# Cluster attention and two MLPs: the preparation of a pair of heads spread to one matmul tile per unit, a second place for the queries' low parts, a third output buffer, and mask halves on two engines

## The chip, the cores and the metric

The kernel runs on one core of a Trainium2 chip. The metric is the time of one execution on the device in microseconds (us). Three executions of the kernel before are shown with their median; one more was profiled.

## The reference, cut to what matters

```python
def _attn_ref(q, k, v, centroids):                    # q, k, v: 2 x 8 x 768 x 64, 16 centroids per head
    q_n, k_n, c_n = (each divided by its norm + 1e-06)
    q_assign = np.argmax(np.einsum('bhsd,hcd->bhsc', q_n, c_n), axis=-1)
    k_assign = np.argmax(np.einsum('bhsd,hcd->bhsc', k_n, c_n), axis=-1)
    mask = q_assign[:, :, :, None] == k_assign[:, :, None, :]
    scores = scale * np.matmul(q, k.transpose(0, 1, 3, 2))
    scores = np.where(mask, scores, -1000000000.0)
    attn = softmax(scores)                            # with 1e-9 added to the sum
    return np.matmul(attn, v)

x = attention as 1536 x 512
x = (sigmoid(x @ w_gate) * (x @ w_val)) @ w_out       # d_ff 1536
x = relu(x @ w_in) ** 2 @ w_out2                      # d_ff 2048
```

A query attends to the keys of its own cluster alone, and the cluster is the centroid of the greatest similarity. Everything is computed to nearly fp32 accuracy: a matrix is held as a high part that TensorE takes in one pass (type F32R) and a low part, the rest.

## The kernel before, in words

The work before the MLPs is 8 pairs of heads (two heads of one batch entry), and each pair is 12 **units**: a head e (two), a half n of the queries (two), and a block j of 128 queries (three). In this text a unit's number is its place in its pair, 0 to 11; the program counts them through, 0 to 95 (`n` in the loop at line 885), and `UPP` is 12.

In a turn of the loop the engines get, in this order: DVE the row maximum of unit n (line 894, `nm<-s`); the copies (`post`) left by the turn before; PE the six transposes of the probabilities of unit n-3 (line 791, `t<-ident,p`), which ACT takes as high parts (793) and DVE as low parts (799, `pt_lo`); PE the scores of unit n+1 (773, `s`); ACT the exponentials (915); DVE the reciprocal of the row sums (844, `nm`) and POOL the normalisation (845, `p`). Then come a third of an attend (`o`, 809 and 810: four matmuls), every third turn with an output copy by ACT (815, `oc`), the sum and split of two heads' outputs on POOL (`finish`: 829, 838 `x_hi`, 840 `x_lo`), the parts of v on POOL (`values`), and last what the tables say for this turn. The matmul tiles of p's transposes and of all preparation come from one pool of three (`ps_t`, name `t`); scores have two, and `o` has one. Each engine works its instructions in the order of this program.

The **preparation** of pair i runs while earlier pairs are in their units. Its pieces are named: `tk0`, `tk1`, `tq0`, `tq1` transpose a half of keys or queries (three transposes, line 551; the high part by ACT, line 556; the low part by DVE, line 557); `s0`, `s1` are four matmuls against the centroids (614); `b0`, `b1` transpose the similarities back (631) and add two of them (641); `am` the maximum over centroids (652), `eq` the comparison with it on DVE (659) and a product on POOL (662), `oh` and `on` a second maximum and the one-hot (669, 675); `mk` six narrow transposes of the one-hot (685), from which ACT makes the row of the mask (695), and DMAs put the row into the operands of the scores (700). `ka`, `kb`, `qa`, `qb` are DMAs that copy parts between the stacked operands of the two heads (596, 600, 602); `load` fetches the inputs of the next pair. All DMAs go out on SP's queue.

`STEPS` names the turn of each piece, counted from the turn ahead of which pair i-1 has its unit 0; `SECOND_STEPS` is for pair 1, and its negative turns stand in the preparation of pair 0, behind its last eight of 17 pieces. A number of -8 to -1 is thus a unit 4 to 11 two pairs ahead of the prepared pair, and 0 to 9 a unit of the pair ahead of it. The low part of the queries has a place of its own (`lo_t["q"]`, from `low_tile`), in one input tile of the MLPs (`x_hi` of the last group) for pairs 0 to 5, and in a tile `lo_q` for pairs 6 and 7. DMAs `qa` and `qb` and the similarities read it. The output copy `oc0` of the first head is held until `finish` has made x_lo of it, some ten units later. Decoding of the first two weights (`early`) is spread over units of the first pairs, on DVE, ACT and POOL.

The stacked operands of pair i and pair i-2 are the same tiles.

Of the kernel before, what the change touches and what calls it, by code (L numbers as in the profile page):

```python
# [8 lines left out]
F32 = mybir.dt.float32  # L9
# [4 lines left out]
AF = mybir.ActivationFunctionType  # L14
ALU = mybir.AluOpType
# [13 lines left out]
STEPS = {  # L29
    -8: ["tq0"],  # L30
    -7: ["tk0"],
    -6: ["tk1"],
    -5: ["tq1", "s0"],
    -3: ["b0", "load"],
    -2: ["s1"],
    -1: ["kb"],
    0: ["qb", "b1"],
    1: ["am"],
    2: ["ka", "qa"],
    3: ["eq"],  # L40
    6: ["oh", "on"],
    7: ["mk"],
}

SECOND_STEPS = {
    -8: ["tk0"],
    -7: ["tq0"],
    -6: ["tk1", "s0"],
    -3: ["tq1"],
    -1: ["s1", "b0"],  # L50
    0: ["b1", "load"],
    1: ["kb"],
    2: ["qb"],
    4: ["am", "ka", "qa"],
    6: ["eq"],
    7: ["oh", "on"],
    9: ["mk"],
}

# [10 lines left out]
def cluster_attention_two_mlps(  # L70
# [13 lines left out]
    nc = tc.nc  # L84
    B, H, S, D = q.shape
    NCL = centroids.shape[1]
    P = 128
# [6 lines left out]
    NH = HB * P  # L94
    NPAIR = H // 2
    scale = 1.0 / float(D) ** 0.5
    TG = 512
    NG = B * S // TG
# [11 lines left out]
    x_in = x_tiles()  # L110
# [199 lines left out]
    with tc.manual_schedule():  # L310
# [12 lines left out]
        rscale = const.tile([4 * NCL, 1], F32, name="rscale")  # L323
        nc.gpsimd.memset(rscale[: 2 * NCL], -1.0)
        nc.gpsimd.memset(rscale[2 * NCL :], -BIG)
        rbias = const.tile([4 * NCL, 1], F32, name="rbias")
# [118 lines left out]
        with ExitStack() as ac:  # L445
# [3 lines left out]
            am = pc.enter_context(tc.tile_pool(name="am", bufs=1, side="right"))  # L449
# [4 lines left out]
            sm = ac.enter_context(tc.tile_pool(name="sm", bufs=6))  # L454
# [78 lines left out]
            Q, K, V = {}, {}, {}  # L533
            factor = {"q": scale, "k": 1.0}

            def prep(i):
# [42 lines left out]
                def low_tile():  # L579
                    if i < len(pairs) - 2:  # L580

                        return x_in[NG - 1][0].rearrange("p k t -> p (k t)")[:, :S]
                    if "hl" not in pools:
                        assert decoded[0] == EARLY and not any(x < N - UPP for x in decoding)
                        early_stack.close()
                        pools["hl"] = sc.enter_context(tc.tile_pool(name="hl", bufs=1))
                    return pools["hl"].tile([P, S], F32R, name="lo_q")
# [94 lines left out]
                def mask():  # L682
                    mt = ps_t.tile([4 * NCL, S], BF16, name="t")
                    for c in range(NB):
                        nc.tensor.transpose(mt[:, c * P : (c + 1) * P], keep["oh"][:, c, :], identb)

                    def post():
                        if i == 0:

                            for t, x in ((K, slice(0, NCL)), (Q, slice(2 * NCL, 3 * NCL))):  # L690
                                nc.scalar.activation(
                                    out=t[i, 0][D : D + NCL, 1], in_=mt[x], func=AF.Identity, scale=rscale[x], bias=rbias[x]
                                )
                        row = am.tile([4 * NCL, S], F32R, name="row")
                        nc.scalar.activation(out=row, in_=mt, func=AF.Identity, scale=rscale, bias=rbias)
                        for e in range(0 if i > 0 else 1, 2):
                            for t, tensor in enumerate((K, Q)):
                                r = slice((2 * t + e) * NCL, (2 * t + e + 1) * NCL)
                                at = D - NCL if e else D
                                nc.sync.dma_start(out=f32(tensor[i, e][at : at + NCL, 1]), in_=f32(row[r]))  # L700

                    return post
# [98 lines left out]
            def attend(i, e, n, third):  # L801

                if third == 0:
                    outs[i, e, n] = ps_o.tile([P, NH], F32, name="o")
                o = outs[i, e, n]
                hi, lo = PThi[i, e, n], PTlo[i, e, n]
                for c in range(third * NB // 3, (third + 1) * NB // 3):
                    vt = V[i, e][:, c].rearrange("p t d -> p (t d)")
                    nc.tensor.matmul(o, vt, hi[:, c, :], start=(c == 0), stop=False)  # L809
                    nc.tensor.matmul(o, vt, lo[:, c, :], start=False, stop=(c == NB - 1))  # L810
                if third == 2:

                    def post():
                        oc = sm.tile([P, NH], F32, name=f"oc{e}", bufs=2)
                        nc.scalar.copy(oc, outs.pop((i, e, n)))  # L815
                        own, other = slice(D * e, D * e + D), slice(D - D * e, 2 * D - D * e)
                        if e == 0:
                            xs[n] = [oc, sm.tile([P, NH], F32, name="x", bufs=2)]
                        nc.sync.dma_start(out=xs[n][1][own], in_=oc[other])
                        if e == 1:  # L820
                            nc.sync.dma_start(out=xs[n][0][own], in_=oc[own])

                    return post
# [61 lines left out]
            for n in range(N + LAG + 4):  # L885
# [10 lines left out]
                if nm is not None:  # L896
                    p = Pt[units[n - 1]]
# [15 lines left out]
                if u is not None:  # L913
                    e = pp.tile([P, S], F32, name="p")
# [92 lines left out]
```

## Time and profile before

| what | value |
|---|---|
| three executions, median (all) | 859.29 us (859.0, 859.29, 859.41) |
| the profiled execution, its own time | 857.28 us |
| its span, first to last instruction | 855.5 us |
| busy in the span: PE, DVE, ACT, POOL | 95%, 73%, 52%, 25% |
| granted TensorE clock, mean | 0.99 |

Engines: PE is TensorE, DVE VectorE, ACT ScalarE, POOL GpSimd, SP the engine whose queue issues the DMAs. The shares are means over attention and MLPs together. "idle before <-X" in a row is the time that the engine stood idle ahead of this instruction and what it then waited for. PE's ends are modelled, so that its busy times overlap.

### The profile page before, as it was taken

How to read it: one execution, taken by the hardware profiler on the slowest of the kernel's cores; microseconds unless marked ns; L12 is line 12 of the kernel's file. 1: busy time of each engine (PE TensorE's matmuls, PEld its weight loads, DVE VectorE, ACT ScalarE, POOL GpSimd, SP SyncE). 2: the span in 40 equal slices, each digit the busy share in tenths (PEclk: the TensorE clock that was granted, in tenths of full speed). 3: DMA queues.
4: the chain of work that ended last, by engine and by line, in shares of the span. 5: the costliest groups of instructions: out<-in, count | busy, mean ns of one | idle time of the engine just before them, and what ended most of it. 6: DMA issues, size and time to landing. Idle time of an engine off the chain costs nothing.

```text
span 855.5 us, 11621 instructions
## 1 busy us (share of the span) xinstructions
PE 816.7 (95%) x4069; PEld 693.1 (81%) x4069; DVE 626.2 (73%) x1143; ACT 446.6 (52%) x888; POOL 213.6 (25%) x347
## 2 busy tenths in 40 slices
PE   6698999999999999999999999999999999999998
PEld 5587988988989878788888888887878888888886
DVE  4598898889888647873678756797675688688533
ACT  6577788888888423343233222344654642652630
POOL 3467888888788110000000000000000000000000
PEclk9799999999999999999999999999999999999999
DMA  5635643643421212121222121211222212222012
GB/s 130 141 70 123 156 103 85 146 106 91 102 68 53 72 47 68 66 81 35 74 74 68 55 66 58 74 50 50 74 75 67 82 49 74 81 68 74 25 50 98
DMA packets 63274, 67.01 MB, mean 78 GB/s; under 512 B 28624, under 2 KB 54224, under 8 KB 63216
## 3 DMA queue, kind: packets, MB, share of 16 engines
q1 hardware_dynamic: 63216, 66.27, 28.2%
q8 instruction: 32, 0.52, 0.3%
q14 instruction: 26, 0.21, 0.1%
HBM read 45.12 MB, written 3.15 MB: 56 GB/s over the span
## 4 chain that ended last, share of the span: by engine, by line
PE 72%; DVE 13%; POOL 5%; ACT 4%; issue 3%; DMA 2%; SPq 0%; DVEq 0%; POOLq 0%; ACTq 0%
PE bank_b L418 16%; PE bank_a L341 12%; PE bank_a L342 12%; PE bank_a L340 12%; PE bank_a L418 9%; DVE pt_lo L799 3%; PE s L773 3%; PE t L791 3%; DVE nm L894 3%; POOL p L845 3%; PE o L809 2%; PE o L810 2%; POOL x_lo L840 1%; DMA st_q<-st_q 1%; PE t L614 1%
## 5 line engine op out<-in xcount | busy, mean ns | idle before, releaser
L342 PE MATMUL bank_a<-x_hi,w 128*128 128x512 f32 x480 | 187.7, 391 | 2.1 <-DVE w L228 2.1
L341 PE MATMUL bank_a<-x_lo,w 128*128 128x512 f32 x480 | 189.3, 394 | 0.3 <-POOL x_lo L840 0.3
L340 PE MATMUL bank_a<-x_hi,w 128*128 128x512 f32 x480 | 188.0, 392 | 0.0
L799 DVE TENSOR_TENSOR pt_lo<-t,pt_hi 128x384 fp32r<-128x384 f32 x192 | 97.6, 545 | 21.7 <-ACT pt_hi L793 20.9
L342 PEld LDWEIGHTS bank_a<-x_hi,w 128*128 128x128 f32 x480 | 90.1, 188 | 22.7 <-DVE w L228 2.5
L340 PEld LDWEIGHTS bank_a<-x_hi,w 128*128 128x128 f32 x480 | 90.1, 188 | 21.0
L341 PEld LDWEIGHTS bank_a<-x_lo,w 128*128 128x128 f32 x480 | 90.1, 188 | 20.4 <-POOL x_lo L840 0.8
L845 POOL TENSOR_SCALAR p<-p,nm,ones 128x768 f32<-128x768 f32 x96 | 96.6, 1006 | 26.5 <-DVE nm L844 24.9
L384 DVE TENSOR_TENSOR slo<-act,shi 128x512 fp32r<-128x512 f32 x84 | 57.4, 687 | 59.1 <-ACT shi L383 54.6
L915 ACT ACTIVATE p<-s,nm 128x768 f32<-128x768 f32 x96 | 88.2, 919 | 16.2 <-DVE nm L844 7.7
L773 PE MATMUL s<-st_k,st_q 128*128 128x384 f32 (+1 forms) x384 | 93.7, 367 | 1.5 <-ACT p L915 0.8
L894 DVE TENSOR_REDUCE nm<-s 128x1 f32<-128x768 f32 x96 | 90.8, 946 | 4.3 <-PE s L773 4.2
L791 PE MATMUL t<-ident,p 128*128 128x128 f32 x576 | 84.5, 281 | 5.5 <-DVE pt_lo L799 3.0
L793 ACT CAST pt_hi<-t 128x384 fp32r<-128x384 f32 x192 | 84.4, 490 | 10.1 <-PE t L791 8.8
L791 PEld LDWEIGHTS t<-ident,p 128*128 128x128 f32 x576 | 69.0, 144 | 14.0 <-ACT sim L620 2.9
L418 PE MATMUL bank_b<-wo,shi 128*128 128x512 f32 x256 | 79.3, 390 | 0.5 <-DVE wo L228 0.5
L383 ACT CAST shi<-act 128x512 fp32r<-128x512 f32 x84 | 51.2, 615 | 52.1 <-PE bank_b L418 27.1
L222 ACT CAST w<-wtop 128x512 fp32r<-128x512 f32 x38 | 23.7, 623 | 102.8 <-DVE wtop L240 102.8
L809 PE MATMUL o<-pt_hi,vt 128*128 128x384 f32 x192 | 66.8, 348 | 7.3 <-ACT oc L815 7.3
L366 DVE TENSOR_TENSOR act<-bank_a,sg 128x512 f32<-128x512 f32 x36 | 24.9, 690 | 66.4 <-PE bank_a L342 60.4
L773 PEld LDWEIGHTS s<-st_k,st_q 128*128 128x128 f32 (+1 forms) x384 | 64.9, 196 | 3.2 <-ACT p L915 1.8
L810 PE MATMUL o<-pt_lo,vt 128*128 128x384 f32 x192 | 65.6, 342 | 0.0
(129 smaller groups left out, 1378.8 us busy)
## 6 DMA issues: line engine op xcount, KB each, us to landing
wraw<-in_moe_w_out_dram SPq DMA_DIRECT2D x28, 512.0 KB, 3.3
wraw<-in_moe_w_in_dram SPq DMA_DIRECT2D x16, 512.0 KB, 3.8
wraw<-in_moe_w_gate_dram SPq DMA_DIRECT2D x11, 512.0 KB, 3.6
wraw<-in_moe_w_val_dram SPq DMA_DIRECT2D x11, 512.0 KB, 3.7
nat_v<-in_v_dram SPq DMA_DIRECT2D x8, 384.0 KB, 3.2
st_k<-st_k SPq DMA_DIRECT2D x16, 192.0 KB, 4.7
x<-oc SPq DMA_DIRECT2D x32, 96.0 KB, 2.1
out_dram<-part SPq DMA_DIRECT2D x12, 256.0 KB, 2.1
```

The costliest lines, as they stand in the source:

```text
L340: nc.tensor.matmul(bk, w[:, 0, ks], mov_hi[:, kk], start=(kk == 0), stop=False)
L341: nc.tensor.matmul(bk, w[:, 0, ks], mov_lo[:, kk], start=False, stop=False)
L342: nc.tensor.matmul(bk, w[:, 1, ks], mov_hi[:, kk], start=False, stop=(kk == KD - 1))
L418: nc.tensor.matmul(bk, st, mv, start=(first and n == 0), stop=(last and n == 2))
L773: nc.tensor.matmul(st[:, m, :NH], Q[i, e][: DEPTH[e][a], a, c * P : (c + 1) * P], K[i, e][: DEPTH[e][a], a, m * NH : (m + 1) * NH], start= ...
L791: nc.tensor.transpose(tp[:, m, :], Pt[u][:, c * P : (c + 1) * P], ident)
L793: nc.scalar.copy(hi, tp)
L799: nc.vector.tensor_tensor(out=lo, in0=tp, in1=f32(hi), op=ALU.subtract)
L809: nc.tensor.matmul(o, vt, hi[:, c, :], start=(c == 0), stop=False)
L845: nc.gpsimd.tensor_scalar(out=p, in0=p, scalar1=nm[:, 3:4], scalar2=ones, op0=ALU.mult, op1=ALU.mult)
L894: nc.vector.tensor_reduce(out=nms[n][:, 0:1], in_=st[n][:, :, :NH], axis=AX.XY, op=ALU.max, negate=True)
L915: nc.scalar.activation(out=e.rearrange("p (m n) -> p m n", m=2), in_=st.pop(n)[:, :, :NH], func=AF.Exp, bias=nms[n][:, 0:1], accum_out=nms ...
```

## The change

The two tables are rewritten, so that no turn has two pieces that take a tile of `ps_t`, and pair 1 has less in front of the first unit and more in units 0 to 5. The low parts of the queries alternate between two tiles for pairs 0 to 5 (`x_hi` and `x_lo` of the last group). Of the two mask halves of pair 0, that of the queries is made on DVE, by a multiplication (its bias is 0), while ACT makes that of the keys. The first head's output copies have three buffers, the second's two as before.

```diff
--- before.py
+++ after.py
@@ -29,31 +29,30 @@
 STEPS = {
     -8: ["tq0"],
     -7: ["tk0"],
-    -6: ["tk1"],
-    -5: ["tq1", "s0"],
+    -6: ["s0"],
+    -5: ["tk1"],
+    -4: ["tq1"],
     -3: ["b0", "load"],
     -2: ["s1"],
-    -1: ["kb"],
-    0: ["qb", "b1"],
-    1: ["am"],
-    2: ["ka", "qa"],
-    3: ["eq"],
-    6: ["oh", "on"],
-    7: ["mk"],
+    -1: ["kb", "b1"],
+    0: ["qb", "am"],
+    1: ["eq"],
+    2: ["oh", "on", "ka", "qa"],
+    3: ["mk"],
 }
 
 SECOND_STEPS = {
-    -8: ["tk0"],
-    -7: ["tq0"],
-    -6: ["tk1", "s0"],
-    -3: ["tq1"],
-    -1: ["s1", "b0"],
-    0: ["b1", "load"],
-    1: ["kb"],
-    2: ["qb"],
-    4: ["am", "ka", "qa"],
+    -6: ["load"],
+    -3: ["tk0"],
+    -2: ["tq0"],
+    -1: ["tk1"],
+    0: ["s0", "tq1"],
+    1: ["s1"],
+    2: ["b0", "kb"],
+    3: ["b1", "qb"],
+    5: ["am"],
     6: ["eq"],
-    7: ["oh", "on"],
+    7: ["oh", "on", "ka", "qa"],
     9: ["mk"],
 }
 
@@ -579,7 +578,7 @@
                 def low_tile():
                     if i < len(pairs) - 2:
 
-                        return x_in[NG - 1][0].rearrange("p k t -> p (k t)")[:, :S]
+                        return x_in[NG - 1][i % 2].rearrange("p k t -> p (k t)")[:, :S]
                     if "hl" not in pools:
                         assert decoded[0] == EARLY and not any(x < N - UPP for x in decoding)
                         early_stack.close()
@@ -687,10 +686,14 @@
                     def post():
                         if i == 0:
 
-                            for t, x in ((K, slice(0, NCL)), (Q, slice(2 * NCL, 3 * NCL))):
-                                nc.scalar.activation(
-                                    out=t[i, 0][D : D + NCL, 1], in_=mt[x], func=AF.Identity, scale=rscale[x], bias=rbias[x]
-                                )
+                            x = slice(2 * NCL, 3 * NCL)
+                            nc.vector.tensor_scalar(
+                                out=Q[i, 0][D : D + NCL, 1], in0=mt[x], scalar1=rscale[x], scalar2=None, op0=ALU.mult
+                            )
+                            x = slice(0, NCL)
+                            nc.scalar.activation(
+                                out=K[i, 0][D : D + NCL, 1], in_=mt[x], func=AF.Identity, scale=rscale[x], bias=rbias[x]
+                            )
                         row = am.tile([4 * NCL, S], F32R, name="row")
                         nc.scalar.activation(out=row, in_=mt, func=AF.Identity, scale=rscale, bias=rbias)
                         for e in range(0 if i > 0 else 1, 2):
@@ -811,7 +814,7 @@
                 if third == 2:
 
                     def post():
-                        oc = sm.tile([P, NH], F32, name=f"oc{e}", bufs=2)
+                        oc = sm.tile([P, NH], F32, name=f"oc{e}", bufs=3 - e)
                         nc.scalar.copy(oc, outs.pop((i, e, n)))
                         own, other = slice(D * e, D * e + D), slice(D - D * e, 2 * D - D * e)
                         if e == 0:
```

Line numbers of the changed kernel are lower by one up to `post` of the mask and higher by three behind it. Its order differs as follows at three places.

On PE, in unit 7 of a steady pair (here pair 3; `oh` is the one-hot of pair 4, `nat_q` the queries' input of pair 5, and `cen` the centroids, for pair 5's similarities), before:

```order
L685 LDWEIGHTS oh
L685 MATMUL t<-identb,oh 64x128
L551 MATMUL t<-ident,nat_q 128x128 x3
L614 MATMUL t<-st_k_142,cen 128x384 x2
L614 MATMUL t<-st_q_144,cen 128x384
L614 MATMUL t<-x_hi_65,cen 128x384
L791 MATMUL t<-ident,p 128x128 x6
L773 MATMUL s<-st_k_143,st_q_145 128x384 x4
L809 MATMUL o<-pt_hi,vt 128x384
L810 MATMUL o<-pt_lo,vt 128x384
```

and pair 5's similarities in the changed kernel, from unit 6 to the next piece:

```order
L613 MATMUL t<-st_k_142,cen 128x384 x2
L613 MATMUL t<-st_q_144,cen 128x384
L613 MATMUL t<-x_lo_66,cen 128x384
L794 MATMUL t<-ident,p 128x128 x6
L776 MATMUL s<-st_k_143,st_q_145 128x384 x4
L812 MATMUL o<-pt_hi,vt 128x384
L813 MATMUL o<-pt_lo,vt 128x384
L812 MATMUL o<-pt_hi,vt 128x384
L813 MATMUL o<-pt_lo,vt 128x384
L550 MATMUL t<-ident,nat_k 128x128 x3
L794 MATMUL t<-ident,p 128x128 x6
```

The similarities follow the first half of the keys now, a whole unit ahead of the next transposes, and the mask stands three units ahead of the similarities, where before mask, transposes and similarities stood in a row between two units' attends.

On DVE at the start, from the totals of pair 0 to the first row maximum, before:

```order
L641 TENSOR_TENSOR tot<-t,part 128x192
L557 SCALAR_TENSOR_TENSOR st_k_142<-t,st_k_142 128x384
L641 TENSOR_TENSOR tot<-t,part 128x192
L652 TENSOR_REDUCE mx<-tot 128x24
L557 SCALAR_TENSOR_TENSOR x_hi_65<-t,st_q_144 128x384
L659 TENSOR_TENSOR eq<-tot,mx 128x384
L662 TENSOR_TENSOR eq<-eq,first 128x384
L557 SCALAR_TENSOR_TENSOR st_k_142<-t,st_k_142 128x384
L669 TENSOR_REDUCE m_306<-eq 128x24
L675 TENSOR_TENSOR oh<-eq,m_306 128x384
L557 SCALAR_TENSOR_TENSOR x_hi_65<-t,st_q_144 128x384
L894 TENSOR_REDUCE nm<-s 128x1
```

and changed:

```order
L640 TENSOR_TENSOR tot<-t,part 128x192 x2
L651 TENSOR_REDUCE mx<-tot 128x24
L658 TENSOR_TENSOR eq<-tot,mx 128x384
L661 TENSOR_TENSOR eq<-eq,first 128x384
L668 TENSOR_REDUCE m_286<-eq 128x24
L674 TENSOR_TENSOR oh<-eq,m_286 128x384
L556 SCALAR_TENSOR_TENSOR st_k_142<-t,st_k_142 128x384
L556 SCALAR_TENSOR_TENSOR x_lo_66<-t,st_q_144 128x384
L690 TENSOR_SCALAR st_q_137<-t,rscale 16x768
L897 TENSOR_REDUCE nm<-s 128x1
```

The low parts of pair 1 (`st_k_142` and the queries') stand behind the one-hot, two of them ahead of the new half of the mask (L690); the other two come after the first row maximum.

On DVE in units 1 to 4 of pair 4 (preparation of pair 5), from the second total to the comparison, before:

```order
L652 TENSOR_REDUCE mx<-tot 128x24
L894 TENSOR_REDUCE nm<-s 128x1
L844 RECIPROCAL nm<-nm 128x1
L799 TENSOR_TENSOR pt_lo<-t,pt_hi 128x3x128 x2
L894 TENSOR_REDUCE nm<-s 128x1
L844 RECIPROCAL nm<-nm 128x1
L799 TENSOR_TENSOR pt_lo<-t,pt_hi 128x3x128 x2
L659 TENSOR_TENSOR eq<-tot,mx 128x384
L894 TENSOR_REDUCE nm<-s 128x1
L844 RECIPROCAL nm<-nm 128x1
L799 TENSOR_TENSOR pt_lo<-t,pt_hi 128x3x128 x2
```

and in units 0 to 3 of the changed kernel:

```order
L651 TENSOR_REDUCE mx<-tot 128x24
L897 TENSOR_REDUCE nm<-s 128x1
L847 RECIPROCAL nm<-nm 128x1
L802 TENSOR_TENSOR pt_lo<-t,pt_hi 128x3x128 x2
L658 TENSOR_TENSOR eq<-tot,mx 128x384
L897 TENSOR_REDUCE nm<-s 128x1
L847 RECIPROCAL nm<-nm 128x1
L802 TENSOR_TENSOR pt_lo<-t,pt_hi 128x3x128 x2
L668 TENSOR_REDUCE m_2278<-eq 128x24
L674 TENSOR_TENSOR oh<-eq,m_2278 128x384
L897 TENSOR_REDUCE nm<-s 128x1
```

The comparison follows the maximum by one unit, not two, and the second maximum and one-hot stand one unit behind it, where before they stood three units later behind a low part.

## Rows read from the trace of the kernel before

**Rows 1.** Stretches of pairs 0 to 5: length, engines' busy time (instructions), granted clock, DMA.

```profile
21.93:60.71 38.78, 29.50 (x158) 26.16 (x157) 29.73 (x58) 23.87 (x54) 19.82 (x30) 0.82 0.42 97
60.71:94.71 34.00, 30.22 (x202) 27.86 (x201) 28.95 (x62) 27.44 (x63) 27.26 (x39) 1.00 0.63 145
94.71:127.29 32.58, 30.21 (x205) 28.27 (x204) 29.78 (x62) 26.56 (x62) 25.78 (x40) 1.00 0.52 117
127.29:159.25 31.96, 29.89 (x200) 27.71 (x199) 27.54 (x59) 26.93 (x63) 28.19 (x42) 1.00 0.48 110
159.25:190.88 31.63, 29.91 (x202) 27.99 (x201) 27.97 (x59) 26.27 (x62) 25.02 (x39) 1.00 0.49 113
190.88:222.48 31.60, 29.88 (x202) 27.93 (x200) 27.96 (x59) 26.27 (x62) 25.28 (x40) 1.00 0.40 94
```

**Rows 2.** Line 894's instructions within 254.3 to 271 us, in pair 7.

```profile
L894 DVE TENSOR_REDUCE nm<-s x9: 945/947/948, 254.4 to 270.7; 128x1 f32<-128x768 f32 x9
```

**Rows 3.** Timeline, PE, pair 5: start, length, instruction.

```profile
217.37 0.49 PE L631 MATMUL t<-ident,sim 128*128 128x128 f32 x3
...
217.70 0.82 PE L791 MATMUL t<-ident,p 128*128 128x128 f32 x6
...
219.76 0.50 PE L614 MATMUL t<-st_k,cen 128*128 128x384 f32 x2
...
220.45 0.82 PE L791 MATMUL t<-ident,p 128*128 128x128 f32 x6
```

**Rows 4.** Timeline, DVE: row maxima of units 1 to 4, 6 and 7, pair 5.

```profile
194.56 0.95 DVE L894 TENSOR_REDUCE nm<-s 128x1 f32<-128x768 f32 x1
...
197.14 0.95 DVE L894 TENSOR_REDUCE nm<-s 128x1 f32<-128x768 f32 x1
...
198.99 0.95 DVE L894 TENSOR_REDUCE nm<-s 128x1 f32<-128x768 f32 x1
...
201.99 0.95 DVE L894 TENSOR_REDUCE nm<-s 128x1 f32<-128x768 f32 x1
...
206.17 0.94 DVE L894 TENSOR_REDUCE nm<-s 128x1 f32<-128x768 f32 x1
...
209.53 0.95 DVE L894 TENSOR_REDUCE nm<-s 128x1 f32<-128x768 f32 x1
```

**Rows 5.** Timeline, DVE: a row maximum of pair 0, two low halves.

```profile
32.19 0.95 DVE L894 TENSOR_REDUCE nm<-s 128x1 f32<-128x768 f32 x1
...
39.38 0.56 DVE L557 SCALAR_TENSOR_TENSOR x_hi<-t,st_q 128x384 fp32r<-128x384 f32 x1 [6.24 <-DMA st_q<-x_hi]
...
75.90 0.56 DVE L557 SCALAR_TENSOR_TENSOR x_hi<-t,st_q 128x384 fp32r<-128x384 f32 x1 [2.79 <-DMA st_q<-x_hi]
```

**Rows 6.** Timeline at the first unit of pair 5: POOL, ACT, PE.

```profile
191.55 1.14 POOL L840 TENSOR_TENSOR x_lo<-oc,x_hi 128x128 fp32r<-128x128 f32 x2
...
192.73 0.48 ACT L815 COPY oc<-o 128x384 f32<-128x384 f32 x1 [1.54 <-POOL x_lo L840]
...
193.26 0.44 PE L809 MATMUL o<-pt_hi,vt 128*128 128x384 f32 x1 [0.82 <-ACT oc L815]
```

**Rows 7.** What line 815 waited for: total us, times.

```profile
  POOL x_lo L840: 11.0, 7
```

**Rows 8.** Timeline of the start: DVE, ACT, PE.

```profile
16.90 0.55 DVE L557 SCALAR_TENSOR_TENSOR st_k<-t,st_k 128x384 fp32r<-128x384 f32 x1
...
17.95 0.56 DVE L675 TENSOR_TENSOR oh<-eq,m 128x384 bf16<-128x384 f32 x1
...
20.18 0.98 ACT L691 ACTIVATE st_q<-t,rbias,rscale 16x768 fp32r<-16x768 bf16 x1
...
21.31 1.30 PE L773 MATMUL s<-st_k,st_q 80*128 80x384 f32 x6 [0.65 <-ACT st_q L691]
```

**Rows 9.** Line 659's instructions: ns shortest, middle, longest.

```profile
L659 DVE TENSOR_TENSOR eq<-tot,mx x8: 547/947/1191, 15.8 to 232.3; 128x384 f32<-128x384 f32 x8
```

**Rows 10.** Stretch of half clock in the first units, columns as in rows 1.

```profile
23.70:30.50 6.80, 6.53 (x25) 6.34 (x25) 4.87 (x10) 4.49 (x12) 5.72 (x10) 0.50 0.79 176
```

## The prediction

> **What bounds the kernel now.** I cut the span at the first row-maximum (line 894) of each pair: [rows 1] are the stretches of pairs 0 to 5, twelve units each. The first begins at 21.93 us. The MLPs that follow pair 7 do not change. In the steady pairs a stretch takes 31.6 us; PE is noted busy for 29.9 of it and DVE for 28.0, so both are close to full and neither alone sets the pace.
>
> PE's busy time overstates its work, because the notes overlap. Its work is better read from starts [rows 3]: from the first `t<-ident,p` (217.70) past scores and attends to the next piece (219.76) a unit issues 2.06 us; three transposes cost 0.33 (217.37 to 217.70), four similarity matmuls 0.69 (219.76 to 220.45). The preparation of a pair is four groups of three transposes of inputs, two of similarities, two of transposes back and six narrow ones of the mask (taken as 0.36): 4 x 0.33 + 2 x 0.69 + 2 x 0.33 + 0.36 = 3.7. So PE's floor is 12 x 2.06 + 3.7 = 28.4 us, 3.2 below the stretch. That units can run at the floor is shown in pair 7, whose units have no preparation: nine row-maxima from 254.4 to 270.7, 2.04 each [rows 2].
>
> DVE has its own lumps [rows 4], as distances between row-maxima of pair 5: unit 1 (totals and maximum) 2.58, unit 2 (nothing extra) 1.85, unit 3 (comparison) 3.00, unit 6 (a low half, second maximum, one-hot) 3.36, or 2.8 without the low half of 0.55 [rows 8]. Where one of these exceeds PE's work of its unit, PE falls behind.
>
> Three waits stand on top. The largest: DVE's low half of the third pair's queries waits 6.24 us for the DMA that still reads the only low place, behind a unit that began at 32.19; again 2.79 us one pair later [rows 5]. Then ACT waits 1.54 us with an output copy for POOL's x_lo, which holds the older copy's buffer [rows 6]; seven times, 11.0 us in all [rows 7], about 1.6 a pair from pair 2 on. And the start: the first scores wait for two mask halves, one after the other on ACT [rows 8].
>
> **The change part by part.** *Start.* Before, three low halves of pair 1 stand on DVE between the totals and the one-hot, as the order shows. They go behind the one-hot; two lie on its chain, 2 x 0.55 = 1.1 us. The second half of the mask, 0.99 on ACT [rows 8], goes to DVE, beside the first. But two low halves stand ahead of it there: one-hot done at 17.4, not 18.5; low halves until 18.5, while PE makes the mask; the half until about 19.4. DVE's new operation (16 x 768 from PSUM) is in no row; the bounds are 0.55 for 384 elements [rows 8] and 0.95 for 768 that line 894 reads from PSUM [rows 4]; I take 0.95, since 768 is its size. First scores complete at about 19.4 to 19.6 instead of 21.3 plus their run: **-1.9**.
>
> What left the start comes back in units 0 to 4: PE gets two groups of similarities and one of transposes, 1.7 us at full clock and 3.4 at half, and the clock is at its lower level, 1.2 GHz (granted 0.50), in 23.7 to 30.5 [rows 10]. DVE gets two low halves, 1.1 us. The bounds are 0 (hidden in the latency of the first units, which have no transposes of p) and 3.4; I take 1.1, DVE's share, because DVE must pass them between two row-maxima: **+1.1**.
>
> *Second low place.* Pair 2 then writes a place whose reader finished before 20 us, so 6.24 and 2.79 go. DVE's own work is not what replaces them: pair 0's stretch has 29.73 us of it in 38.78, pair 1's 28.95 in 34.00 [rows 1]. The drop to half clock that follows the first stall goes with it. **-6.3** in pair 0 and **-2.8** in pair 1. Pairs 6 and 7 share one place still, as before; DVE does not wait there now and its distance to the reader (two units) stays.
>
> *Third buffer.* The copy at a pair's first unit then uses a place that was free for five units; next late there would be POOL's x_lo itself, which only POOL's own queue waits for. PE got 0.8 to 1.1 of ACT's 1.54 as idle time; I take **-1.1** for each of pairs 2 to 7, six times: -6.6. Lower bound 0, if DVE's reciprocal then waits for POOL's nm just as long; upper 1.6.
>
> *The order.* One tile of matmuls per unit removes what units 6 to 8 lose (three tiles in unit 7, and unit 6's lump). But maximum, comparison and one-hot now stand in units 0, 1, 2. By [rows 4] DVE needs 2.58 + 3.00 + 2.8 = 8.4 us there; PE has 3 x 2.06 + 0.33 = 6.5. The excess is 1.9. Before, the same lumps stood apart and cost 3.2 - 1.1 = 2.1 together (floor against stretch, less the output copy). Adjacent lumps share little slack; I keep 1.7 as lost, a gain of 0.4 a pair; bounds 0 and the whole 2.1. Pairs 2 to 5: **-1.6** together. Pair 3 has 0.4 and pair 2 about 1.0 more to lose than pair 5, part of it the early weights on DVE, which stay: **-0.6** for both.
>
> The comparison itself varies: 547 ns alone, 947 in the middle, 1191 at most [rows 9]. It stretches when POOL is at work beside it, and POOL now has values in units 0 and 2 around it. Every steady one is already stretched, so I put no change down. The Trainium skill (SBUF — State Buffer, section SBUF: two separate sides) says that DVE with two SBUF inputs and GpSimd take a shared port pair in turn, each for a whole instruction. The spread agrees. By that rule alone the new place would neither help nor hurt on average.
>
> DMAs: input loads of pair 2 are issued ahead of pair 0's second key half and its two mask rows, which are needed only six units later; no term. Mask rows of a later pair go out four units earlier, ahead of the v load; no term.
>
> Sum: -1.9 + 1.1 - 6.3 - 2.8 - 6.6 - 1.6 - 0.6 = **-18.7**. Against the profiled execution, 857.28 us (span 855.5 and 1.8 around it), that is 838.6. The median is 2.0 above that execution, and I expect the same offset: **840.6 us**.
>
> **The rivals.** *A. The new lumps eat the rest.* If three lumps in a row also delay ACT's exponentials and POOL's normalisation, the 11.0 us of the copy come back as waits of DVE on POOL's nm. For: POOL is busy for 25 to 28 us of each stretch from pair 1 on [rows 1]; in units 11 to 2 it has x_lo, values, its multiply and values again. Against: in pair 5 these leave it 6.3 of 31.6 us free. Only start and low place remain: -1.9 + 1.1 - 6.3 - 2.8 = -9.9, 849.4 us. This is also the case that buffer and order do not do what they say.
>
> *B. The floor is reached.* Buffers between PE and DVE (two score tiles, three transposed ones) could absorb the three lumps, since DVE has spare time in the other nine units. Then pairs 2 to 5 lose 1.7 less each, and pair 6 about 1: -18.7 - 7.8, 832.8 us.
>
> *C. Slower: the clock falls.* PE works less in the start now and its load in the first units is thinner; the granted clock was at half in 23.7 to 30.5 after such a thin stretch [rows 10], and pair 0 has 0.82 in the mean, against 1.00 later [rows 1]. PE's work of such a stretch of 6.8 us costs 3.4 us more at half. With -18.7 on the other side it decides from six such stretches on (6 x 3.4 = 20.4, 861 us). Against: pairs 1 to 5 show 1.00 with PE as full as it will be. The Trainium skill (TensorE: Matmul & The Clock Gate, section What's actually happening) says that the half clock is the default state and activity releases it. By it the first units can again be slow; the later ones, fuller than before, cannot.
>
> **How the numbers follow.** My forecast (837 to 845 around 840.6) has 0.53, A 0.24 (845 to 851), B 0.17 (830 to 837), C 0.04, and 0.02 that gains and losses cancel. A measurement of this kernel tells about 0.2% (1.7 us) from no change: faster 0.95, same 0.01, slower 0.04. The range leaves out C, the outer part of B and of A: **832 to 850**.
>
> **What would show it.** In the trace of the changed kernel: no wait of line 557's successor for a DMA; no ACT wait of the output copy for x_lo; first row-maximum at 20.0, not 21.93; pair 0 about 33.6 us, pair 1 about 31, pairs 4 and 5 about 30.1 each; within them units 0 to 2 as the longest, and PE waiting there for DVE's pt_lo. Wrong would make it: steady stretches still at 31 (A), or at 28.5 (B); a granted clock below 1.00 after pair 0 (C); a first unit later than 21 us; or units 0 to 4 that take over 13 us instead of 10.26 + 1.1.

## The result, and the profile after

The changed kernel takes 837.79 us (median of four executions, 837.05 to 838.98) against 859.20 of the kernel before (859.00 to 859.41): ratio 0.9752, 95% interval 0.9735 to 0.9769, 21.4 us less. Its profiled execution took 837.66 us, span 835.9.

Cut at the same marks as [rows 1], here at line 897, the row maximum of the changed kernel (eight rows now: the last ends at the first matmul of the MLPs). This is the view of windows of the changed kernel, columns as in [rows 1]:

```profile
21.91:54.45 32.54, 29.28 (x172) 25.53 (x172) 30.02 (x60) 24.29 (x56) 20.07 (x31) 0.92 0.39 90
54.45:89.40 34.95, 30.51 (x202) 27.68 (x201) 29.93 (x63) 27.03 (x63) 27.05 (x39) 1.00 0.68 156
89.40:119.76 30.36, 30.06 (x207) 28.40 (x206) 29.69 (x62) 26.45 (x62) 25.90 (x40) 1.00 0.50 114
119.76:149.31 29.55, 28.80 (x197) 27.28 (x196) 27.40 (x59) 26.39 (x63) 27.34 (x42) 1.00 0.50 116
149.31:178.80 29.49, 29.16 (x202) 27.94 (x201) 27.48 (x60) 26.02 (x62) 25.82 (x40) 1.00 0.53 122
178.80:208.14 29.34, 29.05 (x202) 27.90 (x200) 27.45 (x59) 25.96 (x62) 25.29 (x40) 1.00 0.43 99
208.14:235.64 27.50, 27.13 (x183) 25.32 (x181) 25.37 (x55) 24.17 (x55) 23.64 (x37) 1.00 0.36 86
235.64:263.63 27.99, 27.26 (x182) 25.94 (x181) 24.73 (x53) 24.84 (x60) 24.95 (x39) 1.00 0.24 63
```

Against the trace of before (pair 6 had 28.16, pair 7 to the first matmul of the MLPs 32.81), with the prediction's terms beside it:

| stretch | forecast | measured |
|---|---|---|
| start, to the first row maximum | -1.9 | 0.0 |
| pair 0 (low place, less 1.1 for units 0 to 4) | -5.2 | -6.2 |
| pair 1 | -2.8 | +0.95 |
| pairs 2 to 5 (buffer 4 x 1.1, order 2.2) | -6.6 | -9.0 |
| pair 6 | -1.1 | -0.7 |
| pair 7 to the MLPs | -1.1 | -4.8 |
| MLPs | 0 | +0.2 |
| sum | -18.7 | -19.6 |

The sum is right to 1 us, and that closely only by luck, since errors of both signs cancel: two gains did not come (start and pair 1, 5.6 us), and three stretches gave more than forecast (pair 0, pairs 2 to 5, pair 7; 7.1 us). The sum belongs to the two profiled executions, 19.6 us apart. The rest of the distance between the forecast median, 840.6, and the measured one is the offset of 2.0 us between median and profiled execution, which the changed kernel hardly has (837.79 against 837.66).

**The start.** The changed kernel's timeline of DVE, PE and ACT, which answers to [rows 8]:

```profile
17.08 0.56 DVE L674 TENSOR_TENSOR oh<-eq,m 128x384 bf16<-128x384 f32 x1
...
17.70 0.85 PE L684 MATMUL t<-identb,oh 128*64 128x128 bf16 x6 [3.03 <-DVE oh L674]
...
18.65 1.01 DVE L690 TENSOR_SCALAR st_q<-t,rscale 16x768 fp32r<-16x768 bf16 x1
...
19.76 0.98 ACT L694 ACTIVATE st_k<-t,rbias,rscale 16x768 fp32r<-16x768 bf16 x1 [4.57 <-DVE st_q L690]
...
20.89 2.26 PE L776 MATMUL s<-st_k,st_q 80*128 80x384 f32 x6 [0.87 <-ACT st_k L694]
...
21.91 0.96 DVE L897 TENSOR_REDUCE nm<-s 128x1 f32<-128x768 f32 x1 [2.24 <-PE s L776]
```

The one-hot is done at 17.64 in place of 18.51, and the chain then loses all of it: a first unit later than 21 us, one of the prediction's own signs of being wrong, has come. ACT waits for DVE to end its half before it takes the other, so the halves still stand one after the other. And PE, idle for 3.03 us ahead of the mask, works at half clock: from the end of the last half to the row maximum it is 1.17 us in place of 0.77, from the mask's first matmul to the first half 0.95 in place of 0.62. In windows of the changed kernel, the half clock (seventh figure 0.50) reaches over all of this, where before it began at 23.7 [rows 10]:

```profile
13.20:26.85 13.65, 9.74 (x39) 8.43 (x38) 9.02 (x16) 6.53 (x13) 2.99 (x6) 0.50 0.67 151
```

It begins at 13.20, ahead of that idle time, so the idle time alone did not bring it here. In all eleven traces with the new table of pair 1 the clock falls between 12.8 and 18.8 us, ahead of the first scores; with the old one it does so in one of three (the low place alone, at 17.93).

**Pair 1.** The two waits for the low place [rows 5] are gone in both pairs: no low half waits for a DMA any more. But in pair 1 another wait stands at nearly the same place. The changed kernel's timeline of SP, POOL, PE and DVE:

```profile
55.85 0.59 SPq L183 DMA_DIRECT2D spare<-in_moe_w_val_dram  x1
56.54 0.51 SPq L599 DMA_DIRECT2D st_k<-st_k  x1
...
65.92 0.46 SPq L595 DMA_DIRECT2D st_k<-st_k  x1
...
68.75 0.59 SPq L824 DMA_DIRECT2D oc<-oc  x1
...
71.22 1.02 POOL L832 TENSOR_TENSOR oc<-oc,x 128x384 f32<-128x384 f32 x1 [3.39 <-DMA oc<-oc]
...
73.73 0.55 PE L794 MATMUL t<-ident,p 128*128 128x128 f32 x3 [1.30 <-POOL p L848]
...
74.00 0.16 DVE L847 RECIPROCAL nm<-nm 128x1 f32<-128x1 f32 x1 [3.05 <-POOL nm L932]
```

Read it from below: DVE waits 3.05 us for POOL's nm, POOL 3.39 for the copy oc<-oc, which SP issued at 68.75 behind the copies of ka and qa (65.92 and 67.60); those wait for the 384 KB copies of kb and qb, which took 8.5 and 8.4 us to land behind the 512 KB of weights of 55.85. The kernel before has the same wait of POOL beside the stall of 75.90 [rows 5]. It ends 0.96 us behind that stall, and DVE, late itself, feels 0.84 us of it:

```profile
76.86 1.00 POOL L829 TENSOR_TENSOR oc<-oc,x 128x384 f32<-128x384 f32 x1 [3.38 <-DMA oc<-oc]
...
79.62 0.17 DVE L844 RECIPROCAL nm<-nm 128x1 f32<-128x1 f32 x1 [0.84 <-POOL nm L929]
```

**The output copy.** The view of line 818 (815 before), which answers to [rows 7], no longer knows a wait of ACT for x_lo:

```profile
L818 ACT COPY oc<-o x32: 469/480/497, 45.9 to 276.1; 128x384 f32<-128x384 f32 x32
L818 ACTq EVENT_SEMAPHORE  x21: 17/17/38, 88.5 to 275.6; - x21
its engine sat idle before it (us, times) until:
who waited for it (us, times):
  PEld o L812: 0.6, 1
  PE o L812: 0.4, 1
```

The last of the seven waits of before was the dearest, and the prediction gave it no price: its six times 1.1 are the first units of pairs 2 to 7, and the seventh wait stands in the last unit of pair 7. The timeline of the kernel before, from that unit's row maximum, ahead of the MLPs:

```profile
275.59 0.95 DVE L894 TENSOR_REDUCE nm<-s 128x1 f32<-128x768 f32 x1
...
279.16 0.48 ACT L815 COPY oc<-o 128x384 f32<-128x384 f32 x1 [1.52 <-POOL x_lo L840]
...
279.69 0.69 PE L809 MATMUL o<-pt_hi,vt 128*128 128x384 f32 x1 [2.03 <-ACT oc L815]
```

and the same place in the changed kernel:

```profile
258.99 0.95 DVE L897 TENSOR_REDUCE nm<-s 128x1 f32<-128x768 f32 x1
...
260.95 0.47 ACT L818 COPY oc<-o 128x384 f32<-128x384 f32 x1
...
261.47 0.44 PE L812 MATMUL o<-pt_hi,vt 128*128 128x384 f32 x1 [0.40 <-ACT oc L818]
```

Behind its 2.03 us of idle time PE of the kernel before went to half clock for 3.4 us (its windows):

```profile
279.70:283.10 3.40, 3.40 (x13) 3.31 (x14) 1.58 (x3) 1.62 (x5) 0.40 (x1) 0.50 0.12 29
```

From the row maximum of the last unit to the MLPs it takes 7.87 us (275.59 to 283.45), the changed kernel 4.64 (258.99 to 263.63). So of pair 7's 4.8 us the last wait is 3.2, and 1.6 are its other eleven units, the first one's wait among them. The kernel with the tables alone (below) has the same wait, 2.04 us of PE, and its clock stays at full behind it: there this part takes 6.27 us (269.55 to 275.82). So some 1.6 of the 3.2 us are the idle time, and 1.6 the clock. Its windows behind the wait:

```profile
273.66:277.06 3.40, 3.40 (x20) 3.14 (x21) 2.54 (x6) 2.76 (x6) 0.41 (x1) 1.00 0.12 29
```

### The profile page after: what moved, and what is told of

Its sections match the earlier page's. It is cut to its first block, busy times and chain, and to the rows that moved or that the text cites. A ratio compares the mean times of both kernels' runs of the same rounds, so it can differ in the third digit from the quotient of the medians.

```text
span 835.9 us, 11628 instructions
## 1 busy us (share of the span) xinstructions
PE 810.9 (97%) x4069; PEld 689.8 (83%) x4069; DVE 626.1 (75%) x1144; ACT 443.8 (53%) x887; POOL 213.6 (26%) x347
## 4 chain that ended last, share of the span: by engine, by line
PE 77%; DVE 12%; ACT 4%; POOL 3%; issue 2%; DMA 1%; SPq 0%; ACTq 0%; DVEq 0%; POOLq 0%
PE bank_b L417 17%; PE bank_a L340 12%; PE bank_a L341 12%; PE bank_a L339 12%; PE bank_a L417 9%; PE s L776 4%; PE t L794 4%; DVE pt_lo L802 3%; DVE nm L897 2%; PE o L812 2%; PE o L813 2%; POOL p L848 2%; PE t L613 1%; PE t L550 1%; DMA oc<-oc 1%
## 5 line engine op out<-in xcount | busy, mean ns | idle before, releaser
L794 PE MATMUL t<-ident,p 128*128 128x128 f32 x576 | 81.7, 276 | 7.7 <-DVE pt_lo L802 6.0
L794 PEld LDWEIGHTS t<-ident,p 128*128 128x128 f32 x576 | 65.9, 140 | 16.0 <-issue 3.6
L221 ACT CAST w<-wtop 128x512 fp32r<-128x512 f32 x38 | 23.7, 623 | 102.9 <-DVE wtop L239 102.9
L812 PE MATMUL o<-pt_hi,vt 128*128 128x384 f32 x192 | 65.1, 339 | 0.4 <-ACT oc L818 0.4
```

The source lines that it names most:

```text
L794: nc.tensor.transpose(tp[:, m, :], Pt[u][:, c * P : (c + 1) * P], ident)
```

## The experiments

The kernel before ran beside each group on the same chip: 858.08 us with the first four (one part at a time, and two buffers), 858.87 with the next four (one place, the steady table, two mask tiles, the fetch three units later), 856.92 with the last four (medians of nine). The changed kernel was not run again beside them, and one stretch in the MLPs differs from trace to trace by some 2 us (last section). So I read the profiled executions by stretches, and a median "above the changed kernel" is rough; the ratios are to the kernel before.

**One part at a time.** *The third buffer alone*:

```diff
-                        oc = sm.tile([P, NH], F32, name=f"oc{e}", bufs=2)
+                        oc = sm.tile([P, NH], F32, name=f"oc{e}", bufs=3 - e)
```

> The kernel before with the third buffer of the first head's output copies alone. Theory (the buffer's wait is paid on PE at each pair's first unit, and once more in front of the MLPs): the waits of line 815 for x_lo go, PE gains 1.0 to 1.5 us in each of six first units and about 3 us at the end, where PE also keeps its clock; about 850 us, 8 to 10 below the kernel before. Rival (the wait moves on to POOL's small sums, which the reciprocals on DVE wait for): 856 to 859 us.

Measured: 847.33 us, ratio 0.9874 (0.9849 to 0.9900). Pairs 2 to 5 are 1.4 us shorter each, pair 6 1.2, pair 7 to the MLPs 4.7: the theory's mechanism, at the upper end of its size or over it. *The low place alone*:

```diff
-                        return x_in[NG - 1][0].rearrange("p k t -> p (k t)")[:, :S]
+                        return x_in[NG - 1][i % 2].rearrange("p k t -> p (k t)")[:, :S]
```

> The kernel before with the second low place alone. Theory (pair 0's stall of 6.2 us goes wholly, that of 2.8 us in pair 1 is taken over by POOL's wait for copies behind the same long transfers): 852 to 853.5 us. Rival (both go): 850 us; second rival (the next wait on a DMA takes both over): 857 to 859 us.

853.59 us, 0.9950 (0.9934 to 0.9965): pair 0 6.3 shorter, pair 1 only 0.8, as the theory had it. Its timeline shows why: with the old tables, too, POOL's wait stands at the place of the one removed:

```profile
70.02 1.01 POOL L829 TENSOR_TENSOR oc<-oc,x 128x384 f32<-128x384 f32 x1 [2.56 <-DMA oc<-oc]
...
72.80 0.16 DVE L844 RECIPROCAL nm<-nm 128x1 f32<-128x1 f32 x1 [2.89 <-POOL nm L929]
...
73.58 0.92 PE L791 MATMUL t<-ident,p 128*128 128x128 f32 x6 [2.63 <-DVE pt_lo L799]
```

*The two tables alone*, with one low place (for its sake `ka` and `qa` of pair 1 are in turn 4; against the changed table):

```diff
 SECOND_STEPS = {
...
+    4: ["ka", "qa"],
     5: ["am"],
     6: ["eq"],
-    7: ["oh", "on", "ka", "qa"],
+    7: ["oh", "on"],
```

> The kernel before with the two new tables alone, but ka and qa of pair 1 in turn 4, as one low place needs it. One low place, two buffers, both mask halves on ACT. Theory (evenness gives about 1 us in each of pairs 2 to 5, and the earlier loads shorten pair 0's stall to 2 to 3 us): 849 to 852 us. Rival (the tables are most of the gain): 842 to 846 us.

851.88 us, 0.9931 (0.9906 to 0.9957), within the theory. Pairs 2 to 5 are 2.2 us shorter together, which is the -1.6 and -0.6 of the forecast. Pair 6 is 0.8 longer; pair 7's 1.6 less is the clock behind the last wait (above), not the tables. But pair 0 is 4.35 shorter, with the single place: DVE's wait for it is 1.81 us, not 6.24, so the tables and the place remove the same wait.

**One part undone.** *The changed kernel with two buffers* (`bufs=2`):

> The changed kernel with two buffers instead of three. Theory: the waits at the first units and in front of the MLPs return, 846 to 848 us. Rival (in the new order x_lo is ready in time, and the buffer is worth nothing): 838 to 839 us.

851.24 us, 0.9918 (0.9896 to 0.9941): pairs 2 to 6 are 1.4 to 1.8 us longer each, pair 7 to the MLPs 4.85, with half clock in 272.2 to 275.6. That is 13.1 us in these stretches, more than the 11.5 that the buffer gave there alone; the expected 846 to 848 was too little. *The changed kernel with one place* (and `ka` and `qa` of pair 1 in turn 4, as with the tables alone):

```diff
-                        return x_in[NG - 1][i % 2].rearrange("p k t -> p (k t)")[:, :S]
+                        return x_in[NG - 1][0].rearrange("p k t -> p (k t)")[:, :S]
```

> The changed kernel with one low place again (and its step for pair 1's second ka and qa in turn 4, as in the kernel before). Theory: the low place is worth to the changed tables what it is worth to the old ones, 6.3 us of pair 0's stretch, less what the new tables give back by issuing pair 1's second low halves' loads early: pair 0 goes from 32.5 to between 35 and 39 us, pair 1 falls by about 1 us because it can start less late, steady pairs stay at 29.3 to 29.5; time 3 to 5 us above the changed kernel, ratio to the kernel before 0.978 to 0.982. Rival (the parts simply add): 4.5 us above, of which nothing is in pair 1. Second rival (the new tables alone remove the wait for the place): within 1 us of the changed kernel.

839.78 us, 0.9771 (0.9749 to 0.9793): 2.0 above. Pair 0 takes 34.47 in place of 32.54, pair 1 35.19. So the theory and the sum of parts were both too dear: beside the new tables the place is worth 2 us in pair 0, without them 6.3. *The changed kernel with the steady pairs' table of before*:

> The changed kernel with the table of the steady pairs as before, so that of the order only pair 1's table, the start's queue and the places stay. Theory: in the presence of the third buffer the steady table is worth 0.4 to 0.9 us in each of five stretches, because PE's waits of several units vanish together: time 2 to 4.5 us above the changed kernel, stretches of pairs 2 to 6 near 30.2 us as in the kernel that has the buffer alone. Rival: the third buffer alone does it and the table is worth nothing once it is there: within 1 us of the changed kernel, stretches at 29.4.

842.02 us, 0.9799 (0.9778 to 0.9820), 4.2 above: pairs 2 to 5 take 31.15, 30.61, 30.24 and 30.25, 0.75 to 1.06 more each, the upper end of the theory or a little over it. Beside the buffer the table is worth 3.5 us in these four, without it 2.2. Pair 6, the fifth stretch, is the other way: 26.98, 0.52 less with the old table. *The changed kernel with both mask halves on ACT*:

```diff
+                            for t, x in ((K, slice(0, NCL)), (Q, slice(2 * NCL, 3 * NCL))):
+                                nc.scalar.activation(
+                                    out=t[i, 0][D : D + NCL, 1], in_=mt[x], func=AF.Identity, scale=rscale[x], bias=rbias[x]
+                                )
```

> The changed kernel with both halves of pair 0's mask on ACT, as in the kernel before. Theory: splitting the halves over two engines bought nothing, since ACT's half waited for DVE's to end; two halves one after the other on ACT take the same 2 us, and DVE is free a little sooner: first row-maximum at 21.7 to 22.0 us, time within 0.7 us of the changed kernel. Rival (DVE's half did hide, and the start stayed at 21.9 for the clock's sake): first row-maximum at 22.8 to 23.0, time 1 us longer.

836.13 us, 0.9757 (0.9743 to 0.9770), the same ratio as the changed kernel's; the first row maximum is at 21.69. The two halves take 1.98 us on ACT and 2.09 on two engines, so the second engine bought nothing. The clock fell only at 18.48 here, behind the mask's matmuls, and from the first of these to the first half it is 0.62 us, as in the kernel before.

**What holds the halves in a row.** *The mask transposed twice, into two PSUM tiles* (`mq` for DVE's half):

```diff
+                    mq = mt
+                    if i == 0:
+                        mq = ps_t.tile([4 * NCL, S], BF16, name="t")
+                        for c in range(NB):
+                            nc.tensor.transpose(mq[:, c * P : (c + 1) * P], keep["oh"][:, c, :], identb)
```

> The changed kernel, whose first mask is transposed twice by PE, into two PSUM tiles, so that DVE's half and ACT's half read different tiles. Theory: the two halves ran one after the other only because both read one PSUM tile, for which ACT waited for DVE; then ACT's half starts with DVE's, about 0.3 us of PE's work later than before: the first row-maximum ends at 21.2 to 21.4 us in place of 21.91 and the time falls by 0.5 to 0.9 us. Rival: PE at half clock or the DMA rows set the first scores: first row-maximum at 21.9 or later by the added transposes (up to 0.6 us later, as they take 0.85 us at half clock).

835.61 us, 0.9738 (0.9717 to 0.9760). ACT's half now waits for PE, not for DVE, and the two overlap, but the second six transposes delay DVE's: first row maximum at 21.55, 0.36 earlier, less than I had put. *The mask in two tiles by blocks of columns*, no transpose added:

```diff
+                            mts.append(ps_t.tile([4 * NCL, H], BF16, name="t"))
+                            for c in range(NB // 2):
+                                nc.tensor.transpose(mts[h][:, c * P : (c + 1) * P], keep["oh"][:, h * (NB // 2) + c, :], identb)
```

> The changed kernel with pair 0's mask written to two PSUM tiles by block of columns (no transpose is added): ACT takes the keys' part of the first tile while DVE takes the queries' part of the second, and then they change over. Theory: it is the shared tile that put the halves in a row; four operations of 384 elements, two by two, take about 1.1 to 1.3 us in place of 2.1: the first scores start at about 19.8 to 20.1 us in place of 20.7, the first row-maximum at 20.9 to 21.2 in place of 21.91, the time 0.7 to 1.0 us shorter than that of the changed kernel. Rival: the scores' own chain at half clock sets the row-maximum, 21.5 or later as with two whole tiles (21.55).

Its timeline of ACT and DVE:

```profile
18.27 0.66 ACT L699 ACTIVATE st_k<-t,rbias,rscale 16x384 fp32r<-16x384 bf16 x1 [3.34 <-PE t L688]
...
18.73 0.61 DVE L701 TENSOR_SCALAR st_q<-t,rscale 16x384 fp32r<-16x384 bf16 x1
...
19.27 0.60 DVE L704 TENSOR_SCALAR st_q<-t,rscale 16x384 fp32r<-16x384 bf16 x1
...
19.44 0.66 ACT L707 ACTIVATE st_k<-t,rbias,rscale 16x384 fp32r<-16x384 bf16 x1 [0.50 <-DVE st_q L701]
...
21.03 0.96 DVE L914 TENSOR_REDUCE nm<-s 128x1 f32<-128x768 f32 x1 [1.16 <-PE s L793]
```

The halves are done at 20.10 in place of 20.74, and the first row maximum is at 21.03, 0.88 earlier. The clock fell only at 18.82 here, so that some of this could be the clock's; the last run (both edits) settles it, and the shared tile was the cause. The rows show that ACT waits for DVE, not whether the chip or the order that the program builds asks for it. The median, 837.22 us, 0.9764 (0.9749 to 0.9779), can't tell so little.

**What holds pair 1.** *The fetch of 512 KB three units later*, behind the copies of kb and qb (moved from part 5 of the first weight's decoding to part 7):

```diff
-            lower = parts[5]
+            apart = parts[7]
```

> The changed kernel with the second early fetch of weights (512 KB, on the queue of SP) issued three units later in pair 0, behind pair 1's copies of kb and qb instead of ahead of them. Theory: pair 1's chain of waits (the copies land after 8.4 to 8.7 us behind the fetch, the output copies stand behind them on SP, POOL waits 3.4 us for one, DVE 3.1 us for POOL) is made by the fetch; without it pair 1's stretch falls from 34.95 to 31.5 to 32.5 us, and the time by 2 to 3.5 us, ratio to the kernel before 0.971 to 0.973. Rival 1: the decoding of the first weights on DVE sets pair 1's length: within 0.8 us of the changed kernel. Rival 2: the wait moves to the loads of pair 2, which then stand behind the fetch: pair 1 shorter by 2 and pair 2 longer by as much.

838.59 us, 0.9763 (0.9742 to 0.9783). The copies of kb and qb land after 5.3 and 5.1 us, but POOL still waits 3.7 for oc<-oc, and pair 1 takes 35.59. The theory fails: oc<-oc, now issued at 65.52, frees POOL's add only at 71.92, 6.4 us later, against 2.5 in the changed kernel (68.75 to 71.22). Putting the fetch behind the copies of kb and qb only makes the output copies wait in their stead. *The fetch later still, out of that stretch*:

```diff
-EARLY_PARTS = [5, 6, 6, 7, 8, 10, 12, 13, 17, 19, 19, 21, 27, 33, 34, 37, 37, 43]
+EARLY_PARTS = [5, 6, 6, 7, 8, 10, 12, 13, 17, 23, 23, 25, 27, 33, 34, 37, 37, 43]
...
-            lower = parts[5]
+            last = parts[8]
```

> The changed kernel with the second early fetch (512 KB) issued behind the end of the first weight's decoding (pair 1's unit 5, about 75 us) in place of pair 1's unit 0 (55.9), and the second weight's first three parts of decoding moved from pair 1's units 7, 7 and 9 to its units 11, 11 and pair 2's unit 1. Theory: from 56 to 71 us the DMA engines are full (9 in each slice), so pair 1 waits for bytes, whatever their order; with the 512 KB gone, about 2.1 us at the 240 GB/s of that stretch, POOL's wait for the copy oc<-oc falls from 3.4 to about 1.3 and pair 1's stretch from 34.95 to 32.5 to 33.5; pair 2 gets one part of decoding of 1.5 to 2.0 us on DVE and may give 0.5 back: time 1 to 2.5 us shorter than the changed kernel. Rival 1 (the small copies on the queue themselves take the time): wait and stretch as they are, within 0.7 us. Rival 2 (DVE's work of the decoding sets the length): pair 1 shorter by what moved out, pair 2 longer by as much, time within 0.7 us, with POOL's wait shorter or not.

835.27 us, 0.9745 (0.9730 to 0.9759). Pair 1 takes 31.44, pair 2 30.73 (0.37 more), and POOL's add has no wait at all (its timeline, at the same unit as above):

```profile
67.71 0.21 POOL L932 TENSOR_SCALAR nm<-nm 128x1 f32<-128x1 f32 x1
68.01 1.01 POOL L832 TENSOR_TENSOR oc<-oc,x 128x384 f32<-128x384 f32 x1
```

The gain in pair 1, 3.5 us, is more than the 1.5 to 2.5 expected. Two things are in it. POOL's wait stood before any of the moved decoding (its first part was at 78.1 us), so that it went is the fetch's doing. What PE lost in pair 1, as the starts of its instructions above their usual spacing, falls from 2.25 to 0.10 in unit 6, and from 1.30 to 0.96 in unit 7; the 0.64 and 1.28 of units 8 and 10 fall to 0.10, and there the moved work of DVE has a part that this run can't separate. That the DMA engines' share decides is not shown either: it is 0.83 in 56 to 71 us of the changed kernel and 0.86 here. What is shown is which transfers stand ahead of the output copy.

*Both edits*:

> Both edits together, the mask by blocks in two tiles and the late fetch. Theory: they touch stretches that lie 40 us apart and add up: 1.7 to 3.5 us shorter than the changed kernel, 834 to 836 us, ratio to the kernel before 0.971 to 0.973. Rival: an earlier start is given back in pair 1, since the DMA engines are full there until the same time: only as short as the late fetch alone.

834.90 us (833.64 to 835.18), 0.9737 (0.9722 to 0.9751). The first row maximum is at 21.15, pair 1 takes 31.57, pair 2 30.73, all else stands; the profiled span is 831.8, 4.1 below the changed kernel's with MLPs equal to 0.2. The theory of adding up holds by stretches. Here the clock fell at 17.18, ahead of the mask (17.80), so its matmuls ran at half clock as in the changed kernel; yet from the end of the one-hot to the row maximum it is 3.41 us in place of 4.27. So it is the two tiles that bring 0.86. Its timeline of DVE, and its windows over the mask and the first scores:

```profile
17.18 0.56 DVE L674 TENSOR_TENSOR oh<-eq,m 128x384 bf16<-128x384 f32 x1
...
21.15 0.96 DVE L914 TENSOR_REDUCE nm<-s 128x1 f32<-128x768 f32 x1 [1.16 <-PE s L793]
```

```profile
17.20:24.00 6.80, 6.20 (x25) 5.46 (x25) 5.00 (x8) 4.20 (x8) 0.62 (x2) 0.50 0.35 67
```

The ratio's interval overlaps the changed kernel's; on the same chip, the changed kernel with its halves on ACT (0.9757) had 835.92 to 837.06, all above these.

## Why the prediction was right, and where not

**Start, -1.9: wrong, 0.** The DVE half's price held (0.95 taken, 1.01 measured). The step that failed is "The second half of the mask goes to DVE, beside the first": both read one PSUM tile, and ACT's instruction waited for DVE's. Separate tiles brought 0.88 of it back. Most of the rest went to the clock: half clock costs 0.33 us ahead of the halves and 0.40 behind them, and the step put nothing down for it. That PE's work taken out of the start brings the half clock fits the traces (eleven of eleven, against one of three), but is not shown. It would be rival C's mechanism at one place; behind pair 0 the granted clock is 1.00 in every stretch before the MLPs.

**Units 0 to 4, +1.1: too dear.** They take 10.70 us against 10.26, +0.44; but the clock is at full there from 26.85 on, and before it was at half until 30.5, so this is not the price at one clock. Pair 1's own table still has turns with two matmul tiles (`s0` and `tq1` in unit 0; in unit 9 its `mk` meets pair 2's `b0`), unlike what the description of the change says.

**Low place, -6.3 in pair 0: right in size,** shown by the place alone (-6.3). But the new tables alone take 4.35 off pair 0, which the prediction didn't see: it gave them no part in this wait.

**Low place, -2.8 in pair 1: wrong, +0.95 with the tables.** The step that failed is that the whole stall goes away, with DVE's busy time as proof that nothing takes its place. DVE's work did not take it: POOL's wait for oc<-oc did. That wait was there before, 3.38 us long beside the stall and past its end; to find it one had to follow the other engines of that unit, not DVE alone. The late fetch shows what it waited for. The +0.95 itself is loose: in kernels whose edits lie elsewhere (halves on ACT, two mask tiles) pair 1 took 33.82 and 35.37.

**Third buffer, -1.1 a pair: mechanism right, size low.** Alone 1.4 in pairs 2 to 5, beside the new tables 1.6 to 1.8: the upper bound of 1.6 was the nearer. The seventh wait had no term and was worth 3.2: 2 us of PE's idle time stood behind it, and 3.4 us of half clock after that.

**Order, -1.6 and -0.6: right alone (-2.2), low beside the buffer (-3.5 in pairs 2 to 5, by putting the old table back).** In pair 5 the difference is in unit 1 alone: with the old table it gives back 0.22 of what the buffer gains in unit 0 (2.58 us before, 2.80 with the buffer), with the new one nothing (2.44 with two buffers and with three). Why is not shown. In pair 6, where the prediction gave the order nothing, the new table costs 0.5, and so the buffer's -1.2 there comes out as -0.7. Within the order's term, the comparison's price was put down as unchanged. This is the changed kernel's view of the comparison's line, which answers to [rows 9]:

```profile
L658 DVE TENSOR_TENSOR eq<-tot,mx x8: 558/665/756, 15.1 to 212.8; 128x384 f32<-128x384 f32 x8
```

Its middle fell from 947 to 665 ns: in pair 5 it now runs beside the end of POOL's p and its nm (0.66 us), before beside nearly a whole p (from 200.68 us; 1.18). With the old table put back the middle is 966. The rule of the Trainium skill that the prediction weighed (SBUF — State Buffer, section SBUF: two separate sides) agrees so far as in both cases the comparison ends 0.4 us behind that p, but "would neither help nor hurt on average" was my reading of it, and the trace has it otherwise.

**The rivals.** A is refuted: in pairs 3 to 5 DVE waits for POOL's nm for 1.5 us in all (1.2 before), and they take 29.3 to 29.6, not 31. B was nearer than its chance said: 29.34 in pair 5 lies between its floor of 28.4 and my 30.1. Pair 5's units 0 to 2, the three lumps, take 8.13 us (8.4 forecast), but all waits of PE that the trace shows in pair 5 are 0.3 us together.

## What to carry to other kernels

Before a stall is put down as gain, follow each other engine and queue through the same unit: a second wait beside it hardly shows until the first one goes, and then it is the price. If two engines are to share a step, look whether they read the same tile: here they did not overlap until the tile was split. And a wait of PE is worth more than its length where the clock falls behind it: of seven waits of ACT, 1.4 to 1.7 us each, six cost 1.2 to 1.5 us (by the run with the buffer alone), and the seventh 1.6 with the clock at full behind it and 3.2 with the clock at half.

## What the runs showed of the hardware

In all fourteen traces (the kernel before, the changed one, and twelve others) PE sits idle for 2.06 to 2.12 us at one place of the MLPs, waiting for DVE's line 227 or 228. Behind that same wait the clock fell to half for 3.4 us in nine of them, and stayed at full in five. Windows of the kernel with the late fetch, just behind it:

```profile
567.30:570.70 3.40, 3.33 (x8) 2.66 (x9) 3.19 (x7) 0.62 (x1) 0.00 (x0) 0.50 0.50 147
```

and of the changed kernel at the same place of the program:

```profile
570.90:574.30 3.40, 3.40 (x15) 2.80 (x16) 3.19 (x6) 1.42 (x3) 0.00 (x0) 1.00 0.49 150
```

Eight matmuls there against fifteen. The MLPs take 573.6 to 574.2 us in the nine and 571.9 to 572.3 in the five. The same wait led to one clock or to the other, worth 1.8 us of 836, more than several of the terms above. The wait ahead of the MLPs did likewise: 2.03 to 2.04 us of PE in the four traces with two buffers, half clock behind it in three of them. What decides it, no run here tells.
